# Two token blocks loaded on two queues ahead of the start barrier, weight slabs on one queue, dummy matmuls behind both transposes

## The chip, the core and the metric

The kernel runs on one core of a Trainium2 chip. The metric is device time in microseconds (us), the median of several executions. A core has five engines: TensorE (PE; its weight loads, PEld, are shown apart), VectorE (DVE), ScalarE (ACT), GpSimd (POOL) and SyncE (SP). Transfers are issued here from SyncE's and ScalarE's queues.

## The reference

A dense layer, an activation and a second dense layer, in bf16, with S = 2048 tokens, D = 640 and F = 1728:

```
h = jnp.einsum("bsd,df->bsf", x, w1)
h = _silu(h)
out = jnp.einsum("bsf,fd->bsd", h, w2)
```

## The kernel before, in words

TensorE contracts over the partition dimension, so the first product needs x transposed: `xT` holds D on the partitions, in 5 pieces of 128 (DT = 5), and the tokens along the free dimension. The result h is kept transposed as `hT`, with F in 13 full pieces of 128 and a rest of 64 (`hTt`). The second product then uses `hT` directly.

The tokens are worked on in four chunks of 512. For chunks 1 to 3 the transposed x comes from transposing transfers (L142). Chunk 0 would have to wait too long for those, so its four blocks of 128 tokens are loaded as they are into `x0` and transposed on TensorE: `turn(j, b_v, b_a)` (L159 to L181) does five transposes against an identity matrix into PSUM (L166), and copies the result to `xT` on VectorE (L169) and, for blocks 0 and 1, partly on ScalarE (L177).

The start of the program is this. `ahead_of_start` moves an instruction in front of its engine's drain, which precedes the barrier that all engines pass before the kernel proper begins. Before that barrier, SyncE issues the load of token block 0 (L116) and VectorE clears `z`, the operand of the dummy matmuls. Behind the barrier, ScalarE issues the load of the first w1 slab (L119) and then loads its activation table (L129). GpSimd builds the identity. SyncE issues token block 1 (L131), w1 slabs 1 to 4 of the first column group, then the five slabs of the second column group with token blocks 2 and 3 in between, then 15 transposing loads (L142), then w2. A slab is one of the five row pieces of w1, in one of two column groups: columns 0 to 767 (six pieces of 128) or 768 to 1727. Every plain load and store is recorded on L89, in the helper `load`. Each has a semaphore of its own, and the loads of a queue are issued in the order of the program.

TensorE executes in the order of the program. It begins with seven dummy matmuls on `z` (L157; `dummies`, 256 columns each, into a PSUM bank that is used later only after a fresh start), then the transposes of block 0, two more dummies, the transposes of block 1, and then the first real matmuls. `k_outer` goes through column group 0 with the contraction piece k outermost, so that each k needs only the slab with that number; k = 0 and 1 are done for block 0 and block 1 apart (24 matmuls of 128 columns), k = 2 to 4 for both together (18 matmuls of 256 columns). All of these matmuls, like all later real ones, are recorded on L191, in the helper `mm`. Column group 1 follows in the same way, with the transposes of blocks 2 and 3 in between; then the second half of chunk 0, chunks 1 to 3, and the second product with its stores.

ScalarE applies silu out of PSUM (L195). PSUM has eight banks; `bank_free` holds what must be done before a bank is written again.

## Time and profile before

| | |
|---|---|
| median of 6 runs | 127.68 us (127.47 to 128.85) |
| the profiled execution's own time | 128.85 us |
| its span, first to last instruction | 127.3 us |
| TensorE busy | 123.1 us, 97% of the span |
| ScalarE, VectorE busy | 39.4 us, 9.2 us |
| the 63 matmuls that follow block 1's transposes, end to end | 4.67 to 12.83 us |
| first w1 slab, issued on ScalarE's queue | 0.79 us, landing 3.5 us later |
| activation table load | 1.21 to 2.49 us |

The profile is one execution, and all its times count from the first instruction recorded. Its time of 128.85 us is 1.55 us longer than its span, because some work lies around the recorded instructions; it is also the longest of the six. "Landing" is the moment at which a transfer's semaphore is complete. Matmuls overlap in their recorded durations: a row's count divided into its stretch says more about the pace than the mean duration of one.

### The profile page before, as it was taken

Reading aid. Unit: us, or ns where it says so; the run is one execution under the profiler, and the core shown is the slowest. Engines: PE = TensorE matmul, PEld = TensorE weight load, DVE = VectorE, ACT = ScalarE, POOL = GpSimd, SP = SyncE. Lnnn points to the kernel's source line nnn. Section 1 sums busy time; section 2 is a strip of 40 time slices with the busy share of each in tenths; the row PEclk is TensorE's granted clock in tenths of the full one; section 3 lists DMA queues with packets and bytes.
Section 4 is the critical chain, followed back from the end, with each engine's and each line's share of the span. In section 5 each row is a group of like instructions: output and inputs, shape, how many; then the busy total and the mean of one; then the engine's idle time right before and its main releaser. Section 6 shows DMA issues by size and latency. Waiting matters only on the chain.

```text
span 127.3 us, 1539 instructions
## 1 busy us (share of the span) xinstructions
PE 123.1 (97%) x670; PEld 63.9 (50%) x680; DVE 9.2 (7%) x16; ACT 39.4 (31%) x69; POOL 0.8 (1%) x7
## 2 busy tenths in 40 slices
PE   7799999999999999999999999999999999999994
PEld 4678888444444444444444443444344444444452
DVE  0100300000000000000000004202020201022021
ACT  5104466455555555555550003010101011010100
POOL 2000000000000000000000000000000000000000
PEclk9999999999999999999999999999999999999999
DMA  5999644459900000000000000442102111111113
GB/s 133 347 377 218 79 98 107 93 98 341 347 14 0 0 0 0 3 5 0 0 0 0 0 0 0 88 120 105 64 27 76 51 51 57 51 51 51 51 51 103
DMA packets 16646, 10.37 MB, mean 81 GB/s; under 512 B 10880, under 2 KB 16640, under 8 KB 16640
## 3 DMA queue, kind: packets, MB, share of 16 engines
q1 hardware_dynamic: 16352, 10.02, 27.7%
q10 hardware_dynamic: 288, 0.26, 0.6%
q8 instruction: 5, 0.08, 0.3%
q14 instruction: 1, 0.01, 0.0%
HBM read 5.16 MB, written 2.62 MB: 61 GB/s over the span
## 4 chain that ended last, share of the span: by engine, by line
PE 95%; DMA 3%; issue 1%; ACT 0%
PE ps L191 94%; DMA x<-in_x_dram 3%; PE ps L166 1%; ACT o_sb L322 0%
## 5 line engine op out<-in xcount | busy, mean ns | idle before, releaser
L191 PE MATMUL ps<-xT,w1s 128*128 128x512 bf16 (+3 forms) x353 | 61.3, 344 | 0.2
L191 PEld LDWEIGHTS ps<-xT,w1s 128*128 128x128 bf16 (+1 forms) x357 | 34.7, 104 | 26.0 <-ACT hT L195 0.4
L191 PE MATMUL ps<-w2s,hT 128*128 128x512 bf16 (+2 forms) x217 | 45.1, 367 | 0.3 <-issue 0.2
L195 ACT ACTIVATE hT<-ps 128x512 bf16<-128x512 f32 (+1 forms) x53 | 30.5, 590 | 28.9 <-PE ps L191 28.9
L191 PEld LDWEIGHTS ps<-w2s,hT 128*128 128x128 bf16 x221 | 20.9, 98 | 24.5 <-issue 1.1
L322 ACT CAST o_sb<-ps 128x512 bf16<-128x512 f32 (+1 forms) x8 | 4.4, 545 | 42.2 <-PE ps L191 42.2
L191 PE MATMUL ps<-hT,w2s 128*128 128x512 bf16 x50 | 11.1, 379 | 0.2 <-issue 0.2
L320 DVE CAST o_sb<-ps 128x512 bf16<-128x512 f32 (+1 forms) x9 | 6.1, 677 | 39.9 <-PE ps L191 39.9
L191 PEld LDWEIGHTS ps<-hT,w2s 128*128 128x128 bf16 x52 | 5.0, 98 | 6.3 <-issue 0.4
L320 DVE CAST oT<-ps 128x512 bf16<-128x512 f32 x2 | 1.3, 686 | 63.4 <-PE ps L191 63.4
L322 ACT CAST oT<-ps 128x512 bf16<-128x512 f32 x2 | 1.1, 588 | 11.1 <-PE ps L191 11.1
L157 PE MATMUL ps<-z 128*128 128x256 bf16 x9 | 2.3, 412 | 0.8 <-PEq L430 0.8
L166 PE MATMUL ps<-ident,x 128*128 128x128 bf16 x20 | 2.3, 265 | 0.7 <-DMA x<-in_x_dram 0.7
L169 DVE COPY xT<-ps 128x384 bf16<-128x384 bf16 (+1 forms) x4 | 1.7, 425 | 12.7 <-PE ps L166 12.7
L166 PEld LDWEIGHTS ps<-ident,x 128*128 128x128 bf16 x20 | 1.6, 117 | 1.6 <-DMA x<-in_x_dram 1.4
L191 PE MATMUL ps<-w2t,hTt 64*128 64x512 bf16 (+2 forms) x17 | 2.2, 366 | 0.0
L157 PEld LDWEIGHTS ps<-z 128*128 128x128 bf16 x9 | 1.1, 138 | 1.1 <-issue 0.8
L129 ACT ACT_TABLE_LOAD x1 | 1.3, 1283 | 1.2 <-PEq L430 1.2
L195 ACT ACTIVATE hTt<-ps 128x512 bf16<-128x512 f32 x2 | 1.2, 597 | 1.1 <-PE ps L191 1.1
L191 PEld LDWEIGHTS ps<-w2t,hTt 64*128 64x128 bf16 x17 | 0.7, 94 | 1.4 <-issue 0.8
L177 ACT COPY xT<-ps 128x256 bf16<-128x256 bf16 x2 | 0.7, 372 | 1.8 <-PE ps L166 1.8
L191 PE MATMUL ps<-hTt,w2t 64*128 64x512 bf16 x4 | 0.6, 382 | 0.0
(10 smaller groups left out, 1.5 us busy)
## 6 DMA issues: line engine op xcount, KB each, us to landing
out_dram<-o_sb SPq DMA_DIRECT2D x15, 160.0 KB, 1.8
w1s<-in_w_dram SPq DMA_DIRECT2D x5, 240.0 KB, 4.5
w2s<-in_w_dram SPq DMA_DIRECT2D x1, 1120.0 KB, 6.3
w2s<-in_w_dram SPq DMA_DIRECT2D x1, 960.0 KB, 9.4
w1s<-in_w_dram SPq DMA_DIRECT2D x4, 192.0 KB, 3.8
x<-in_x_dram SPq DMA_DIRECT2D x2, 160.0 KB, 2.8
x<-in_x_dram SPq DMA_DIRECT2D x1, 320.0 KB, 5.2
xT<-in_x_dram SPq DMA_TRANSPOSE x15, 3.4
```

Of the source, the lines that this page charges most:

```text
L129: act.activation(out=warm[:, :], in_=warm[:, :], func=ACT.Silu)
L157: pe.matmul(ps[:, 3, 0:HB], lhsT=z[:, 0:P], rhs=z[:, :], start=True, stop=True)
L166: ins = pe.transpose(dst, x0[:, j, dt * P:(dt + 1) * P], ident[:, :])
L169: r = tick(dve.tensor_copy(out=xT[:, 0:nv, j * P:(j + 1) * P], in_=v[:, 0:nv * P].rearrange("p (k s) -> p k s", s=P),), s_dve)
L177: r = tick(act.copy(out=xT[:, nv:DT, j * P:(j + 1) * P], in_=a[:, 0:(DT - nv) * P].rearrange("p (k s) -> p k s", s=P),), s_act)
L191: return pe.matmul(o, lhsT=l, rhs=r, start=start, stop=stop, skip_group_check=shared)
L195: r = tick(act.activation(out=out_ap, in_=in_ap, func=ACT.Silu), s_act)
L320: r = tick(dve.tensor_copy(out=out_ap, in_=in_ap), s_dve)
L322: r = tick(act.copy(out=out_ap, in_=in_ap), s_act)
```

## The change

Token block 1 is issued on ScalarE's queue ahead of the barrier, beside block 0 on SyncE's queue. The first slab of w1 moves from ScalarE's queue to SyncE's, where it takes the place of block 1. On TensorE the transposes of block 1 follow directly on those of block 0, and the two dummy matmuls come after both. The number of transfers, of dummies and of every other instruction stays the same. Line numbers behind the change are smaller by one (L191 becomes L190).

```diff
         ld_x[0] = ahead_of_start(lambda: load(sp, x0[:, 0, :], x_v[:, 0, :]), ET.SP)
+        ld_x[1] = ahead_of_start(lambda: load(act, x0[:, 1, :], x_v[:, 1, :]), ET.Activation)
         ahead_of_start(lambda: dve.memset(z[:, :], 0.0), ET.DVE)
 
-        ld_w1[0, 0] = load(act, w1s[:, 0, c0g[0]:c1g[0]], w1_v[:, 0, c0g[0]:c1g[0]])
         act_warm = pool.memset(warm[:, :], 0.0)
...
-        ld_x[1] = load(sp, x0[:, 1, :], x_v[:, 1, :])
-        for k in range(1, DT):
+        for k in range(DT):
             ld_w1[0, k] = load(sp, w1s[:, k, c0g[0]:c1g[0]], w1_v[:, k, c0g[0]:c1g[0]])
...
         dummies(7)
         t0 = turn(0, 7, 6)
+        t1 = turn(1, 5, 4)
         dummies(2)
-        t1 = turn(1, 5, 4)
```

## The prediction

> **What bounds the kernel now.** I read the chain of waits first, then the start of the timeline by engine, then the transfers, then the pace of the matmuls.

> The chain that ended last, in order of time (start, length, what):

> ```profile
> by line: PE ps L191 93.7%; DMA x<-in_x_dram 2.6%; PE ps L166 1.0%; issue 0.7%; ACT o_sb L322 0.2%
> ...
> 0.79 3.32 DMA x<-in_x_dram
> 4.12 0.05 issue
> 4.16 0.72 PE ps L166 x5
> 4.88 7.95 PE ps L191 x63
> ```

> TensorE is the bound from 4.16 us to the end. Only one other thing is on the chain: token block 1, issued at 0.79 and landed 3.3 us later. After 4.16 no slab, copy or store interrupts the matmuls for more than 0.16 us. The change edits only this opening, so at most about 4 us can move, unless it also changes the pace of what follows.

> The opening on TensorE and the loads on SyncE's queue (timeline, start and length):

> ```profile
> 0.84 1.65 PE L157 MATMUL ps<-z 128*128 128x256 bf16 x7 [0.84 <-PEq L430]
> 2.28 0.74 PE L166 MATMUL ps<-ident,x 128*128 128x128 bf16 x5
> 2.81 0.63 PE L157 MATMUL ps<-z 128*128 128x256 bf16 x2
> 4.16 0.72 PE L166 MATMUL ps<-ident,x 128*128 128x128 bf16 x5 [0.72 <-DMA x<-in_x_dram]
> 4.67 5.54 PE L191 MATMUL ps<-xT,w1s 128*128 128x128 bf16 x39
> ```

> Seven dummies end at 2.28, just as block 0 is there (its landing is 2.2). Its transposes take 2.28 to 2.81, two dummies follow, and then TensorE waits for block 1. The page calls that hole 0.72; a dummy here occupies only 0.21 (seven in 1.44), so the last one stops issuing near 3.24, and the hole is nearer 0.92.

> Landings, from the issue rows in two stretches (0 to 0.7 us, 0.7 to 1.15 us):

> ```profile
> x<-in_x_dram SPq DMA_DIRECT2D x1, 160.0 KB, 2.2
> ...
> w1s<-in_w_dram ACTq DMA_DIRECT2D x1, 192.0 KB, 3.5
> x<-in_x_dram SPq DMA_DIRECT2D x1, 160.0 KB, 3.3
> ```

> A load issued alone lands in 2.2 us; two issued together on two queues take 3.3 and 3.5.

> The pace, by stretches of the same 256-column matmuls (columns: length, then busy and count for PE, PEld, DVE, ACT and POOL, then PEclk, DMA share, GB/s):

> ```profile
> 7.30:9.30 2.00, 2.00 (x12) 1.44 (x10) 0.00 (x0) 0.00 (x0) 0.00 (x0) 1.00 1.05 373
> 10.00:12.00 2.00, 2.00 (x20) 1.79 (x19) 0.00 (x0) 1.57 (x3) 0.00 (x0) 1.00 1.35 210
> ```

> This is the most important view. The same instruction goes 12 times into one stretch and 20 times into the other (each count has about two still draining at an edge). That is 0.21 us against 0.11 us each, without any wait. Narrower stretches put the switch near 9.6 us. Everything TensorE does before 9.6 runs at half pace.

> [...] PEclk reads 1.00 in both rows. By that column the pace is fixed, and a microsecond of wait removed saves a microsecond. [...] If real work starts at S and the gate opens at O, the stretch from S to O does half the work, so the end moves by (change of S + change of O)/2. Before: S = 4.67, O = 9.6. [...] Starting earlier with O unchanged is worth only half. [...]

> **The change, part by part.**

> *Block 1 goes to ScalarE's queue, ahead of the barrier.* It is issued about 0.1 us after block 0 instead of at 0.79. Its issue costs ScalarE about 0.38 (the length of the ACTq row). Today SyncE's issue and drain release the barrier near 0.7; ScalarE, a little later, may delay that by up to 0.1 us. Queued behind it are the dummies (they fill a wait anyway), the slab loads, and the table load. The table load is 1.28 us, starts 0.4 us sooner than now because slab 0's issue no longer precedes it, and feeds a copy first needed near 3.5. So nothing there is on the path.

> *What the two blocks do to each other.* The trace never shows two loads from an idle start. Low bound: each lands as block 0 does today, 2.2, with block 1 behind it at 2.6. High bound: both behave as today's pair, 3.3 and about 3.6. [...] I take 2.8 for block 0 and 3.0 for block 1.

> *Slab 0 takes block 1's old place on SyncE; slabs 1 to 4 keep their issue times.* The queue rows are as many as before (one x out, one slab in, 0.34 against 0.42 us each), so everything after shifts by at most 0.1 us. Slab 0: low bound is 0.52 us of transfer at the 371 GB/s seen from 2.7 to 3.2 us, behind the two blocks, hence landing 3.6; high bound is today's 3.5 us after issue, hence 4.35.

> *The two dummies move behind block 1's transposes.* Today they cost nothing, since the hole hides them. Now they stand between the last transpose and the first matmul: 0.43 us at half pace on the path wherever slab 0 has landed. They are free only if slab 0 comes last. The copies of block 0 (0.36 us, starting about 0.25 after its last transpose) lie beside block 1's transposes.

> The sum for S: transposes of block 0 from 2.8, 0.53; of block 1, 0.53; dummies 0.43; S = 4.3. Slab 0, 3.6 to 4.35, lands beside that. Against 4.67 this is 0.37 sooner. Bounds: blocks at 2.2 and 2.6 give 2.28 + 0.53 + 0.53 + 0.43 = 3.8; blocks at 3.3 and 3.6 give 3.3 + 1.06 + 0.43 = 4.8, which is 0.13 later than now.

> For O: the unbroken feed of TensorE starts at 4.16 today, and at 2.8 after. With the same lag to the release O moves by 1.36. [...]

> The likeliest sum: (0.37 + 1.36)/2 = 0.87 us. Later stages do not take it back: the second group of slabs lands at 7.4, 8.0, 8.5, 10.3 and 10.9 and blocks 2 and 3 at 9.7, while TensorE asks for the first near 8.5 even if the gate opened at 6.2 (group 0 is 24 matmuls of 0.055 and 18 of 0.11, 3.3 us at full pace; 0.95 of it is done from 4.3 to 6.2), then for one more every 7 x 0.11 = 0.76 us, 0.8 us or more behind each landing. From there every stage is the same matmuls at the full pace.

> The profiled execution took 128.85 us, 1.55 more than its span of 127.3, and is the longest of the six; the median is 127.68. Its sum gives 127.98; applied to the median, 126.8. The 1.2 us between that run and the median are themselves the size of a gate that opened 2.3 us later, so the median run may have less to gain than the profiled one.

> **The rivals.**

> [...] Chance 0.17.

> *The gate does not move; only the wait goes.* (0.37 + 0)/2 = 0.19, 127.5 us; with S at its bounds 127.2 to 127.75. [...] Chance 0.34. Within 0.5% (0.64 us) is about what a measurement of this kernel can tell from no change.

> *Slower: block 0 late, a wider hole, a lost window.* Only seven dummies cover block 0, and they end near 2.3. If its company delays it to 3.3, the hole before the first transpose is 1.0 us instead of 0.92, and the 0.43 us of dummies then lie on the path. S is later than 4.67 as soon as block 0 lands after 3.18. The price in S is little: 0.13/2. [...] Chance 0.19.

> *The likeliest, gate and start both move:* 126.8, chance 0.30.

> **The numbers.** Faster by over 0.5%: 0.30 + 0.17 = 0.47. Within: 0.34. Slower: 0.19. The range reaches from the whole window, 125.7, to the beginning of the slow case, 128.5, because no trace shows where the gate opens in the median run. The likeliest faster case alone spans 126.2 to 127.1.

> **What would show it.** Two x rows issued before 0.2 us, landing 2.8 and 3.0; ten transposes back to back; the first L190 matmul (today's L191) near 4.3; the count of 256-column matmuls in two microseconds changing from 12 to 20 well before 9.6. Wrong: block 0 landing after 3.2; a second hole waiting for slab 0; the change of pace still near 9.6; or a wait for a slab in the second group.

## The result, and the profile after

| | before | after |
|---|---|---|
| median of all executions | 127.92 us (72, from 126.23 to 129.26) | 126.91 us (35, from 126.47 to 129.21) |
| executions above 128 us | 34 of 72 | 3 of 35 |
| span of the profiled execution | 127.3 us | 125.5 us |

The ratio after to before is 0.9957, with a 95% interval of 0.9942 to 0.9973: faster by 0.43%. This ratio leaves out, on both sides, executions more than 1.5% above the fastest of their kernel; in the kernel before that is the later part of its wide spread, 31 of 72 executions, to which the profiled one, with its change of pace at 9.6 us, belongs, so the gain by the ratio is smaller than that by the medians (0.992). The forecast was 126.8 us and faster by 0.7% of the median known then. The time was met; by the ratio the gain is about 0.6 of the forecast one, and the way there is not the one that was forecast.

The opening on TensorE after the change (timeline: start, length, operation, count, and in brackets the idle time before it and what ended it):

```profile
0.97 1.65 PE L156 MATMUL ps<-z 128*128 128x256 bf16 x7 [0.97 <-PEq L429]
2.41 1.27 PE L165 MATMUL ps<-ident,x 128*128 128x128 bf16 x10
3.48 0.63 PE L156 MATMUL ps<-z 128*128 128x256 bf16 x2
4.53 6.09 PE L190 MATMUL ps<-xT,w1s 128*128 128x128 bf16 x63 [0.42 <-DMA w1s<-in_w_dram]
10.54 0.45 PE L165 MATMUL ps<-ident,x 128*128 128x128 bf16 x5
```

Both blocks are there in time: ten transposes run back to back from 2.41. The first real matmul starts at 4.53 instead of 4.67, so the wait has hardly become shorter. It has changed hands: it now waits for slab 0. The group of 63 matmuls that took 8.16 us before takes 6.09.

The three first loads (from issue to landing):

```profile
w1s<-in_w_dram SPq DMA_DIRECT2D x1, 192.0 KB, 3.5
x<-in_x_dram SPq DMA_DIRECT2D x1, 160.0 KB, 2.4
x<-in_x_dram ACTq DMA_DIRECT2D x1, 160.0 KB, 2.7
```

Block 0 pays 0.2 us for block 1's company, and block 1 lands at 2.8 instead of 4.1. Slab 0, issued at 0.93, still takes 3.5.

The pace (stretches; length, then busy and count for PE, PEld, DVE, ACT and POOL, then PEclk, DMA share, GB/s):

```profile
5.20:6.20 1.00, 1.00 (x19) 1.00 (x20) 0.00 (x0) 0.00 (x0) 0.00 (x0) 1.00 0.97 328
7.30:9.30 2.00, 2.00 (x21) 1.79 (x19) 0.00 (x0) 1.38 (x3) 0.00 (x0) 1.00 1.01 350
```

From 7.30 to 9.30 there are 21 matmuls of 256 columns where there were 12. In this execution the full pace is there from the first real matmul: the trace's list of clock changes begins at 4.39 us here, and at 9.62 in the kernel before. "The gate opens", in the prediction, the expectations and below, is a name for this change alone: from 256-column matmuls 0.21 us apart to 0.11 us apart.

The chain of waits, shares and some of the pieces from the barrier to chunk 1:

```profile
PE ps L190 89%; DMA w1s<-in_w_dram 5%; SPq L89 3%; PE ps L165 0%; ACT o_sb L321 0%
...
4.63 0.49 SPq L89
5.16 5.92 DMA w1s<-in_w_dram
11.12 0.94 PE ps L190 x7
12.06 0.28 PE ps L165 x5
12.34 7.86 PE ps L190 x72
20.25 10.74 PE ps L190 x49
```

Before, TensorE carried the chain from 4.16 us on. Now the slabs carry it up to 11.12: TensorE has caught up with them. The slab issued at 5.16 is the last but one of w1. From 20.25 on, where the first matmul of 512 columns is recorded, nothing differs: 105.28 us are left in this profile and, from 22.06, in the one of before (127.34 - 22.06).

### The profile page after: what moved, and what is told of

It reads as the page before. It is cut to its first block, busy times and chain, and to the rows that moved or that the text cites. A ratio compares the mean times of both kernels' runs of the same rounds, so it can differ in the third digit from the quotient of the medians.

```text
span 125.5 us, 1539 instructions
## 1 busy us (share of the span) xinstructions
PE 121.2 (97%) x670; PEld 62.1 (49%) x680; DVE 9.2 (7%) x16; ACT 39.4 (31%) x69; POOL 0.8 (1%) x7
## 3 DMA queue, kind: packets, MB, share of 16 engines
HBM read 5.16 MB, written 2.62 MB: 62 GB/s over the span
## 4 chain that ended last, share of the span: by engine, by line
PE 89%; DMA 5%; SPq 3%; issue 1%; ACT 0%
PE ps L190 89%; DMA w1s<-in_w_dram 5%; SPq L89 3%; PE ps L165 0%; ACT o_sb L321 0%
## 5 line engine op out<-in xcount | busy, mean ns | idle before, releaser
L190 PE MATMUL ps<-xT,w1s 128*128 128x512 bf16 (+3 forms) x353 | 59.1, 333 | 0.9 <-DMA w1s<-in_w_dram 0.4
L190 PEld LDWEIGHTS ps<-xT,w1s 128*128 128x128 bf16 (+1 forms) x357 | 32.6, 98 | 27.0 <-DVE xT L168 0.9
L190 PE MATMUL ps<-w2s,hT 128*128 128x512 bf16 (+2 forms) x217 | 45.1, 367 | 0.3 <-issue 0.2
L190 PEld LDWEIGHTS ps<-w2s,hT 128*128 128x128 bf16 x221 | 20.9, 98 | 24.4 <-issue 1.1
L190 PE MATMUL ps<-hT,w2s 128*128 128x512 bf16 x50 | 11.1, 379 | 0.2 <-issue 0.2
L190 PEld LDWEIGHTS ps<-hT,w2s 128*128 128x128 bf16 x52 | 5.0, 98 | 6.3 <-issue 0.4
L190 PE MATMUL ps<-w2t,hTt 64*128 64x512 bf16 (+2 forms) x17 | 2.2, 366 | 0.0
L190 PEld LDWEIGHTS ps<-w2t,hTt 64*128 64x128 bf16 x17 | 0.7, 94 | 1.4 <-issue 0.8
L190 PE MATMUL ps<-hTt,w2t 64*128 64x512 bf16 x4 | 0.6, 382 | 0.0
## 6 DMA issues: line engine op xcount, KB each, us to landing
w1s<-in_w_dram SPq DMA_DIRECT2D x5, 192.0 KB, 4.0
```

The costliest lines, as they stand in the source:

```text
L190: return pe.matmul(o, lhsT=l, rhs=r, start=start, stop=stop, skip_group_check=shared)
```

## The experiments

Two theories stood at the start. **The gate:** what counts is how busy TensorE is kept before its real work, because that decides when the pace changes from 0.21 to 0.11 us (when the gate opens); the loads matter since they shorten the hole. **The wait alone:** what counts is when the first real matmul can start. They differ most where one edit changes only the dummies. Medians are of all executions; kernels of one batch ran on one chip, beside the kernel before, whose median was 127.92 at first, then 128.57 (E1 to E4), 128.21 (E5 to E8) and 127.75 (E9 to E12).

**E1, the loads alone.** As after, with the dummies where they were.

```diff
+        dummies(2)
         t1 = turn(1, 5, 4)
-        dummies(2)
```

> Only the loads are moved; the two dummies stay between the transposes of block 0 and block 1. Theory A (the gain is the clock gate's release coming sooner, because the loads leave TensorE no long hole before its real work): first real matmul within 0.3 us of the 4.53 of the changed kernel (slab 0 sets it), but the idle stretch just before it is longer, 0.8 to 1.0 us instead of about 0.6, so the release is late in more executions: median 127.0 to 127.5. Rival B (only the wait for block 1 counts, dummies are idle filling): the same as the changed kernel, 126.9 within 0.15.

Measured: 126.97 us (126.76 to 127.46), ratio 0.987 (0.983 to 0.991), first real matmul at 4.54. It is as the changed kernel: where the two dummies stand makes no difference that these six executions show, once the loads are early. I had expected the hole before the real work to be longer and the release later. It was not longer, about 0.5 us: dummies between the transposes push block 1's transposes back to 3.56, and these end near 4.0.

**E2, the dummies alone.** The kernel before, with the dummies behind both transposes.

```diff
-        dummies(2)
         t1 = turn(1, 5, 4)
+        dummies(2)
```

> Only the two dummies are moved behind block 1's transposes; all loads as before. Theory A: the hole on TensorE before block 1 grows from 0.9 to 1.35 us and the two dummies stand on the path, so the release comes no sooner and the start 0.3 to 0.4 later: median 128.1 to 128.5. Rival C (it is dummies directly before the real work that open the gate): faster than before, 127.0 to 127.4.

Measured: 128.91 us (127.91 to 129.53) beside 128.57, above the 128.1 to 128.5 that I expected. The ratio is 1.0064 (1.0019 to 1.0109), but the medians of all executions are only 0.3% apart, inside the spread of either kernel. So it is not faster, and slower is not shown. TensorE's timeline:

```profile
2.28 0.74 PE L166 MATMUL ps<-ident,x 128*128 128x128 bf16 x5
4.28 0.71 PE L166 MATMUL ps<-ident,x 128*128 128x128 bf16 x5 [1.26 <-DMA x<-in_x_dram]
4.79 0.63 PE L157 MATMUL ps<-z 128*128 128x256 bf16 x2
5.21 6.97 PE L191 MATMUL ps<-xT,w1s 128*128 128x128 bf16 x59
```

The transposes end issuing at 2.81, so the hole is 1.47 us. The dummies are no longer hidden, and the start moves to 5.21. In this profile the spacing of the matmuls changes at 8.6; the two dummies next to the real work alone brought no gain in the median.

**E3, the hole filled.** The kernel before, not one load moved, four more dummies.

```diff
-        dummies(2)
+        dummies(6)
         t1 = turn(1, 5, 4)
```

> The kernel before with six dummies instead of two in the hole, no load moved: TensorE is kept busy from 0.84 us to about 4.1. First real matmul unchanged near 4.67. Theory A: the gate opens near or before 5 us instead of 7 to 10, and the median falls to 126.3 to 127.0 without any change of the loads. Rival B (the removed wait for block 1 is the gain): the wait is still there, so 127.9 within 0.2.

Measured: 126.69 us (six executions, 126.34 to 127.62) beside 128.57, ratio 0.985 (0.980 to 0.990). This alone gives as much as the moved loads do beside it (E1, 0.987). The wait for block 1 is still there (its transposes start at 4.42, later than before, and real work at 4.93 instead of the expected 4.67), so the theory of the wait alone falls. The spacing changes at 5.3 in this profile. The slabs were late by themselves in it:

```profile
4.93 3.00 PE L191 MATMUL ps<-xT,w1s 128*128 128x128 bf16 x36
8.40 3.13 PE L191 MATMUL ps<-xT,w1s 128*128 128x256 bf16 x27 [0.47 <-DMA w1s<-in_w_dram]
```

**E4, no dummies at all.** The changed kernel without both calls.

```diff
-        dummies(7)
         t0 = turn(0, 7, 6)
         t1 = turn(1, 5, 4)
-        dummies(2)
```

> The changed kernel without any dummy, so TensorE does its first instruction when block 0 has landed, near 2.3 us. First real matmul near 4.4 to 4.5, as in the changed kernel. Theory A: the unbroken feed starts at the first real matmul, the gate opens at 7 to 9 us, and the median is 128.0 to 129.0. Rival B: as the changed kernel or 0.05 sooner, 126.8 to 127.0.

Measured: 128.46 us (127.0 to 130.37) beside 128.57. The first real matmul started at 4.44 in its profile, sooner than in the changed kernel, and the kernel is 1.5 us slower than E1 beside it. The early loads without the dummies are worth nothing in the median of all executions, and by the ratio 0.4% (0.9959, 0.9929 to 0.9989). The profiled execution is the fastest of the 22: the spacing of its matmuls changes at 6.1.

**E5, the changed kernel filled.**

```diff
-        dummies(2)
+        dummies(5)
```

> The changed kernel with five dummies instead of two behind block 1's transposes, so TensorE is busy until about 4.3 and its hole before the first real matmul is closed. If the gate theory holds and the slab stream is the bound once the gate is open: the few executions above 128 us disappear, but the median stays at 126.7 to 126.95, since the slabs land when they do. If the gate still limited the changed kernel's median: 126.3 or less.

Measured: 127.05 us (126.49 to 127.61, 12 executions) beside 128.21. No execution is late, but neither is any of the 20 of the unaltered changed kernel in E12, so the five dummies cannot be credited with that. The median does not improve (it is 0.1 above the expected range, on a chip on which the unaltered changed kernel did not run). So the gate no longer seems to limit the changed kernel's median; E12 gives a better ground for this.

**E6, one queue.** Both blocks on SyncE, ahead of the barrier.

```diff
-        ld_x[1] = ahead_of_start(lambda: load(act, x0[:, 1, :], x_v[:, 1, :]), ET.Activation)
+        ld_x[1] = ahead_of_start(lambda: load(sp, x0[:, 1, :], x_v[:, 1, :]), ET.SP)
```

> The changed kernel with block 1 issued behind block 0 on SyncE's queue, both ahead of the barrier; no load on ScalarE's queue. The barrier comes 0.3 us later (a second issue of 0.39 ahead of the drain), and so do dummies and slabs. Block 0 lands at 2.2 instead of 2.37, block 1 at 2.7 to 3.0. If the second queue is what helps: slab 0 lands at 4.6 to 4.7, the end moves by the slab stream's 0.3: median 127.2. If only being ahead of the barrier matters: 126.9 within 0.15.

Measured: 127.03 us (126.78 to 127.27). The barrier is 0.34 us later (first dummy at 1.31), block 1 lands at 2.76, slab 0 at 4.32, although it is issued at 1.27. That is within the range expected if only being ahead of the barrier matters. The second queue is not what helps.

**E7 and E8, the slabs by themselves.** After and before, with TensorE waiting for the last slab ahead of all real work.

```diff
+        wait(pe, ld_w1[1, 4])
         h_done = {}
```

> The changed kernel in which TensorE waits for the last w1 slab before its first real matmul, so that it reads nothing from SBUF while the slabs arrive. Its time is several us longer and not of interest; what counts is when the slabs land. If TensorE at full pace is what delays the slabs: the last lands at 10.9 or sooner instead of 11.74. If it is the order and the later issue of the loads: 11.5 to 11.9.

> The same wait in the kernel before. If TensorE's reading delays slabs, its half pace did so little: the last slab lands near 10.9 or a little sooner. If the order of the loads is the cause, the last slab lands 0.5 us or more before that of the changed kernel with the same wait.

Measured: the last slab of E7 (issued at 5.61) and the last two of E8 (issued at 5.00 and 5.57; both take about 5.0) in the rows of issues, E7 first:

```profile
w1s<-in_w_dram SPq DMA_DIRECT2D x1, 240.0 KB, 5.8
```

```profile
w1s<-in_w_dram SPq DMA_DIRECT2D x2, 240.0 KB, 5.0
```

With TensorE silent the last slab lands at 11.40 with the new loads and at 10.61 with the old. With TensorE working it was 11.74 and 10.94. So the slabs are 0.8 us later with the new loads whether TensorE works or not. TensorE's reading is not the cause: in E11, below, it works at full pace beside the old loads, and the last slab lands at 10.61 too. In seven profiles with the new loads (after, E1, E4 to E7, E12) it landed at 11.2 to 11.7, in four with the old (before, E2, E8, E11) at 10.6 to 10.9, and only E3's own delay (12.3) falls outside.

E7 gave something else. In its 7.5 us of silence (3.90 to 11.45) the granted clock fell from 1.00 to 0.50 (the gate closed), and the clock column shows it (same columns as above):

```profile
7.90:8.20 0.30, 0.00 (x0) 0.00 (x0) 0.00 (x0) 0.00 (x0) 0.00 (x0) 1.00 0.99 354
8.22:8.52 0.30, 0.00 (x0) 0.00 (x0) 0.00 (x0) 0.00 (x0) 0.00 (x0) 0.50 1.04 361
14.70:15.00 0.30, 0.30 (x3) 0.22 (x2) 0.00 (x0) 0.00 (x0) 0.00 (x0) 0.50 0.78 182
15.05:15.35 0.30, 0.30 (x4) 0.28 (x3) 0.00 (x0) 0.00 (x0) 0.00 (x0) 1.00 0.78 168
```

**E9, slab 0 back on ScalarE's queue.** The changed kernel otherwise.

```diff
+        ld_w1[0, 0] = load(act, w1s[:, 0, c0g[0]:c1g[0]], w1_v[:, 0, c0g[0]:c1g[0]])
         act_warm = pool.memset(warm[:, :], 0.0)
...
-        for k in range(DT):
+        for k in range(1, DT):
```

> The changed kernel with slab 0 back on ScalarE's queue, behind the barrier. If moving slab 0 to SyncE's queue is what makes the slabs late: the last slab lands at 10.6 to 11.0 instead of 11.2 to 11.7, and the median falls to 126.4 to 126.7. If block 1's early load is the cause, or it is neither: last slab 11.3 to 11.8, median 126.9 within 0.15.

Measured: the last slab at 10.71, as expected; the median 127.31 beside 127.75 (ratio 0.9959, 0.9928 to 0.9989), not as expected. The executions fall into two heaps: 12 from 126.28 to 127.31 and 10 from 128.56 to 129.73.

```profile
2.44 1.25 PE L166 MATMUL ps<-ident,x 128*128 128x128 bf16 x10
3.48 0.44 PE L157 MATMUL ps<-z 128*128 128x256 bf16 x2
5.07 5.76 PE L191 MATMUL ps<-xT,w1s 128*128 128x128 bf16 x63 [1.15 <-DMA w1s<-in_w_dram]
```

Slab 0 now lands only at 4.93, beside slab 1 at 4.74, and TensorE has a hole of 1.2 to 1.4 us. In this profile the gate had opened at 3.58, just ahead of the hole, and the real matmuls run at full pace (22 of them in the row from 5.30 to 6.30, where E2 has 12); the second heap, 1.2 us and more above the first, is where I place the executions in which the gate opened only behind the hole. The profile shows only an execution of the first, so this is not shown.

**E10, the same, filled** with five dummies.

> As the one before, with five dummies behind block 1's transposes so that TensorE has no hole before the first real matmul. If slab 0's queue matters and the gate then limits again: 126.2 to 126.5, with no execution above 127.5. Otherwise as the one before.

Measured: 127.23 us (126.53 to 128.9), ratio 1.0001 (0.9977 to 1.0025), first real matmul at 5.09. The upper heap is nearly gone, with one execution of 22 above 128.1, but the median gains nothing and the expected 126.2 to 126.5 is missed: slab 0 is as late as in E9 (4.96). The loads are those of E9, yet the last slab lands at 11.29. The rows of its issue, at 5.13 in E9 and at 5.14 in E10:

```profile
w1s<-in_w_dram SPq DMA_DIRECT2D x1, 240.0 KB, 5.6
```

```profile
w1s<-in_w_dram SPq DMA_DIRECT2D x1, 240.0 KB, 6.2
```

So E9's early last slab does not show that slab 0's queue decides. In E10 most of the delay comes in one step: slabs 3 and 4 of the first group land at 5.79 and 7.32, 1.5 us apart, against 0.5 in E9. E3 has such a step too, with the old loads (6.37 to 8.35).

**E11, the hole half filled.** The kernel before with two more dummies.

```diff
-        dummies(2)
+        dummies(4)
         t1 = turn(1, 5, 4)
```

> The kernel before with four dummies in the hole instead of two (six closed it and gave 126.69 beside 128.57). The hole shrinks from 0.9 to about 0.5 us, as wide as the one that the changed kernel has. If the gate tolerates a hole of that width: median as with six, 126.5 to 127.0. If it needs an unbroken feed: half way, 127.4 to 128.0.

**E12, the changed kernel again**, beside E9 to E11.

> The changed kernel unaltered, beside the three others on the same chip: 126.9 within 0.15, last slab at 11.2 to 11.8 again if its lateness belongs to the order of the loads, about 10.9 if the first profile only happened to show it late.

Measured: E11 126.78 us (126.34 to 127.58), ratio 0.9956 (0.9931 to 0.9981); E12 127.02 us (126.42 to 127.36), ratio 0.9983 (0.9960 to 1.0006), its last slab at 11.65 again. On this chip the ratio does not show the change to be faster; the medians (127.02 beside 127.75) and the spread do. Two more dummies in the kernel before, without any moved load, are at least as good as the change; the two are not clearly apart. E11's opening:

```profile
2.81 1.06 PE L157 MATMUL ps<-z 128*128 128x256 bf16 x4
4.26 0.45 PE L166 MATMUL ps<-ident,x 128*128 128x128 bf16 x5 [0.39 <-DMA x<-in_x_dram]
4.55 5.83 PE L191 MATMUL ps<-xT,w1s 128*128 128x128 bf16 x63
10.22 0.44 PE L166 MATMUL ps<-ident,x 128*128 128x128 bf16 x5
```

It starts real work at 4.55, as the changed kernel does at 4.53, at full pace, and is hardly held up by a slab (0.06 us): it reaches the 512-column matmuls at 19.40. After's first such matmul is missing from its trace, but its weight load is there, at 20.04.

E12's profile shows the changed kernel with a later gate:

```profile
4.71 6.47 PE L190 MATMUL ps<-xT,w1s 128*128 128x128 bf16 x63 [0.51 <-DMA w1s<-in_w_dram]
```

```profile
5.00:6.00 1.00, 1.00 (x12) 1.00 (x11) 0.00 (x0) 0.00 (x0) 0.00 (x0) 1.00 1.02 301
```

The row from 5 to 6 us counts 12 matmuls, where that of after counts 19 from 5.2 to 6.2: E12 is still at half pace, and the spacing changes at 6.25. It then waits for no slab, and reaches the 512-column matmuls at 20.19. In E4, E5 and E6 the spacing changes at 6.1 to 6.2, and they get there at 20.0 to 20.1. So with the new loads it makes no difference whether the gate opens at 4.4 or at 6.2: what is gained at the gate is lost again waiting for slabs. That is why closing the hole (E5) brings nothing.

## Why the prediction was right and where it was wrong

**Right: the view of the opening and the formula.** The end moves by half of (change of S + change of O), since matmuls between S and O run at half pace (those of 256 columns 0.21 us apart instead of 0.11). With the gate open before real work, O counts as S. S is the start of real work, O the opening of the gate, by the trace's list or by the change of spacing. For six profiles, against before (S 4.67, O 9.6, half sum 7.13), with the waits for slabs behind S added:

| | S | O | half sum against before | waits for slabs | sum | span against before |
|---|---|---|---|---|---|---|
| after | 4.53 | S | -2.60 | 0.65 | -1.95 | -1.81 |
| E12 | 4.71 | 6.25 | -1.65 | 0 | -1.65 | -1.65 |
| E2 | 5.21 | 8.6 | -0.23 | 0 | -0.23 | -0.20 |
| E3 | 4.93 | 5.3 | -2.02 | 0.64 | -1.38 | -1.22 |
| E9 | 5.07 | S | -2.06 | 0 | -2.06 | -1.99 |
| E11 | 4.55 | S | -2.58 | 0 | -2.58 | -2.44 |

The 0.65 of after is its time from S to the weight load of the first 512-column matmul (15.51 us) less that of E11 (14.85); the 0.64 of E3 is the gap in its matmuls from 7.65 to 8.40, less one matmul. The sums come within 0.2 us, and those of E4, E5, E6 and E10 within 0.05. The waits of after, on TensorE's weight loads:

```profile
5.17 5.17 PEld L190 LDWEIGHTS ps<-xT,w1s 128*128 128x128 bf16 x57 [0.32 <-DMA w1s<-in_w_dram]
10.54 0.28 PEld L165 LDWEIGHTS ps<-ident,x 128*128 128x128 bf16 x5 [0.20 <-DMA x<-in_x_dram]
11.12 0.66 PEld L190 LDWEIGHTS ps<-xT,w1s 128*128 128x128 bf16 x7 [0.29 <-DMA w1s<-in_w_dram]
```

**Right, with a size: the gate.** What fills the hole changes when it opens. With no load moved it opened at 9.6 with a hole of 0.92 us (before) and at 8.6 with one of 1.47 (E2), but ahead of 4.55 with four dummies in the hole (E11) and at 5.3 with six (E3); so the width of the hole alone does not give the moment. How large a hole may be is an estimate of mine, from E7's distances of 3.41 and 6.83 us between clock changes and from the pace of what was issued: it takes the same 3.41 us for every profile, and works out the busy share of each window that ended at a listed clock change, or a whole number of windows away from one. Windows with 0.57 (E2), 0.71 (E8) and 0.73 (before, 2.80 to 6.21) left the gate closed; windows with 0.73 (E7), 0.76 (E9), 0.81 (E1), 0.86 (after) and 0.94 (E6) opened it. So by this estimate it took about three quarters of a window in these profiles; 0.73 went either way. The hole of before, 0.92 us, leaves 0.73 to any window that holds all of it, just on that edge. I take this as the reason why its executions spread over 3 us; no run shows that it is. The hole of after, from 3.90 to 4.53, leaves 0.81, and nearly all its executions lie together. That share is worked out from few profiles, and that every profile has windows of 3.41 us was not shown; the edge itself was not measured more closely, and which executions opened early was seen only in profiled ones.

**The steps that failed.** The first is the size of one term: "With the same lag to the release O moves by 1.36". No run shows a lag of one length from the start of the unbroken feed to the release: it is 5.4 us in before (4.16 to 9.6), 4.3 in E2 (4.28 to 8.6) and 0.9 in E3 (4.42 to 5.3). O moved by 3.4 us, to 6.25 in E12 and to 6.1 to 6.2 in E4 to E6; in after it opened even ahead of S, 5.1 us sooner in the formula. By the estimate above E6 is the nearest comparison: the window that ended at 6.21 in before was 0.73 busy and the gate stayed closed, the one that ended at 6.20 in E6 was 0.94 busy and the gate opened. The opening differs with what fills the hole, and not by a lag of one length behind the start of the feed.

The second is the base: 0.87 us, worked out from a profiled execution whose gate opened at 9.6, was taken off the median. By the same formula the gate of an execution at the median of 127.92, 0.93 us shorter than the profiled one, opens near 7.8 (an estimate, 9.6 less twice 0.93). I had written that the median execution may have less to gain than the profiled one, and did not put it into the number. Against the profiled execution the forecast was 127.98, and the profiled one of after took 127.01.

The third is "Later stages do not take it back". I asked whether TensorE would meet the slabs with their landings of before, 0.8 us or more ahead of each demand. The landings moved: the last slab comes at 11.74 instead of 10.94. After waits at slab 1, at block 2 and at the last but one slab, and gives 0.65 us back. Where the gate opens at 6.2 nothing is given back, but nothing more can be gained either: the slabs set a floor. The fastest of 35 executions of after took 126.47 us, the fastest of 72 of before 126.23.

What makes the slabs late stays open. From 5 to 8 us the same loads of the same queue moved 365 GB/s with the old order and 321 with the new one, with TensorE silent in both (E8, E7). Slab 0's queue does not settle it: with slab 0 back on ScalarE's queue the last slab landed at 10.71 in one profile and at 11.29 in the other (E9, E10), and each kernel has one profile.

**Smaller misses.** The start: I gained 0.37 on S, it was 0.14. No run shows the landings of 2.8 and 3.0 from which S was added up: blocks 0 and 1 came at 2.37 and 2.78. I had read the 195 GB/s that moved in before from 1.0 to 1.9 us, where block 0 moved, as a limit for two blocks; with both under way, and slab 0 behind them, 333 GB/s moved from 1.5 to 2.0 us in after. The second queue itself gave nothing that the runs show: with both blocks on one queue (E6) block 1 landed at 2.76 and the median was 127.03, beside 2.78 and 126.91 with two. Slab 0 came at 4.39, past the bound of 4.35, and sets S; the two dummies therefore cost nothing.

**Why the sum looked right.** The median of all executions fell by 1.0 us and I had 0.87. That is luck: O moved too little, and the whole gain was taken off the median; the two errors cancelled. Among the earlier executions of before there was less to gain, and the floor weighs fully: 0.43%, not 0.7%.

**The rivals.** That the gate does not move (127.5) is refuted by the profiles and by the narrower spread. The whole window, near 125.8 us, to which I gave a chance of 0.17, means a gate that opens 3.4 us sooner, at 6.2; the profile of before had no evidence for that length, and E7's distance of 3.41 us came later. The opening is what the profiles show: O at 6.1 to 6.25 in E4, E5, E6 and E12. Its 1.9 us, (0.37 + 3.4)/2, taken off the profiled execution instead of the median, give 126.95, and 127.01 was measured, though in that execution the gate opened earlier still and the slabs took 0.65 us back. The slower case, with a late block 0 and a later opening, did not come about: block 0 landed at 2.37. E2, with a hole of 1.47 us and its gate open at 8.6, and the late heap of E9 (128.56 to 129.73) point to a price of a wide hole without showing it.

## What to carry to other kernels

Where TensorE's first microseconds run at half pace (0.21 us instead of 0.11 between 256-column matmuls here), find the holes in its work before asking what the loads could do: a few dummies that bridge the hole gave here what rearranging the loads gave (E3 and E11 against the change). After any gain at the start of a stage ask again when the next operand lands in the changed kernel, not in the old one. And look at the spread of the executions as well as at their median: I read 3 us of spread here as a sign that the opening of the gate differed from one execution to the next, and two profiles of the changed kernel do show it at 4.39 and at 6.25 us. A gain that is read from one profiled execution holds for that execution; ask where it lies among the others before taking it off the median.

## What the runs showed of the hardware that was not expected

A clock column at 1.00 can mean "no change recorded yet": before's matmuls of 256 columns were 0.21 us apart under it, and E7's 0.50 has the same pace. E7's clock changes lie 3.41 and 6.83 us apart. Its first, at 4.80, came although TensorE had been idle for the 0.90 us before it (from 3.90), so the gate opened there without an unbroken feed. A load of 192 KB that was issued first behind the barrier took 3.5 us to land on SyncE's queue (after), and 4.0 us on ScalarE's beside slab 1 on SyncE's (E9), although two loads of 160 KB issued together from an idle start took 2.4 and 2.7.
